# Decode attention over 65,536 keys: K transposed on VectorE in 32x32 blocks of bf16 pairs, scores and V as 512-column products, 32 KB load rows

## Chip, cores, metric

One core of a Trainium2 chip. The metric is device microseconds (us) per execution. One of the runs of the kernel before took 745 us, far from all others; it is in no ratio, but it is one of the four behind the median of 707.1 us below. In the profiles, PE is TensorE's products, PEld its weight loads, DVE VectorE, ACT ScalarE, SPq the sync engine's queue that issues the loads. PSUM is the memory that the kernels' products are written to and added up in. Of a product's two operands the code calls the stationary one (the weights) lhsT and the moving one rhs. L148 is a line of the kernel's file.

## The reference, cut

```python
B, Hq, Hkv, Sq, Sk, D = 1, 32, 8, 1, 65536, 128          # all bf16
k = jnp.repeat(k, 4, axis=1); v = jnp.repeat(v, 4, axis=1)
scores = jnp.einsum("bhqd,bhkd->bhqk", q, k) * D ** -0.5
out    = jnp.einsum("bhqk,bhkd->bhqd", softmax(scores), v)
```

One query per head, eight groups of four heads. Each group reads 16.8 MB of K and 16.8 MB of V, 268.4 MB in all, and does little arithmetic with them. K arrives with keys on the partitions. In both kernels a product contracts over the partitions of its two operands, and the score product contracts over d, so both transpose K.

## The kernel before

K and V are read in blocks of 16,384 keys (4 MB) into four shared buffers. For each K block TensorE makes 128 transposes, VectorE copies them out of PSUM eight at a time, and TensorE makes 128 products with four columns each. For each V block it makes 128 more. In the source, K blocks of one group are interleaved with V blocks of the group before it, eight chunks of 128 keys at a time.

```python
KB = 16384; T = 32; CB = 4                 # a partition's share of a block: 4 runs of 32 keys = 4 x 8 KB
iopool = tc.tile_pool(name="iopool", bufs=4)            # K and V blocks share the buffers
nc.sync.dma_start(out=kn, in_=k[0, g, b*KB:(b+1)*KB, :].rearrange("(c p t) d -> p c t d", p=P, t=T))
# K step, per 8 chunks
for i in range(8):
    nc.tensor.transpose(out=pt[:, i*P:(i+1)*P], in_=kn[:, c, t0+i, :], identity=ident_bf)   # L148
nc.vector.tensor_copy(out=kTn, in_=pt)                                                      # L154
for i in range(8):
    nc.tensor.matmul(out=sc[:, 4*jj:4*jj+4], lhsT=kTn[:, i*P:(i+1)*P], rhs=qT_g)            # L157
# V step, per chunk
nc.tensor.matmul(out=psum_oT, lhsT=vb[:, c, t, :], rhs=E_g[:, 4*j:4*j+4])                   # L195
# ... cut: maximum over the group, exp on ScalarE, row sums, normalisation at the end
```

## Time and profile before

| | before |
|---|---|
| time, us | 706.9 (703.7 to 707.3 without the outlier) |
| span of the profiled run, us | 705.8 |
| mean load rate over the span | 380 GB/s |
| load rate while loads are queued | 425 GB/s |
| PE / DVE busy | 80% / 56% |

Three lines of the profile's page: the share of 16 DMA engines and the rate in 40 equal slices of the span, and the chain of waits, by engine. The chain is the work that ended last, followed back step by step to what released it.

```profile
DMA  8999799997989979899799997989979899799994
GB/s 332 427 425 425 305 405 387 386 426 327 423 356 391 426 319 425 353 397 421 308 423 377 404 420 321 423 358 425 427 309 408 360 393 423 325 413 386 425 427 202
...
PE 67%; DVE 20%; issue 6%; ACT 5%; DMA 2%; SPq 0%; DVEq 0%; ACTq 0%
```

The rate reaches 425 GB/s and then dips, deepest once in about five slices (88 us), which is once per group. Stretches of 2 us round the first group change show a dip from near. The last three columns are the granted TensorE clock (1.00 is full), the DMA share and the rate.

```profile
80.00:82.00 2.00, 1.90 (x44) 1.76 (x43) 1.77 (x4) 0.69 (x2) 0.00 (x0) 1.00 0.99 422
82.00:84.00 2.00, 2.00 (x74) 1.96 (x71) 1.21 (x3) 0.00 (x0) 0.00 (x0) 1.00 0.56 233
84.00:86.00 2.00, 2.00 (x78) 2.00 (x74) 0.00 (x0) 0.00 (x0) 0.00 (x0) 1.00 0.04 16
86.00:88.00 2.00, 2.00 (x49) 2.00 (x46) 1.38 (x2) 0.00 (x0) 0.00 (x0) 0.59 0.03 8
88.00:90.00 2.00, 1.41 (x26) 1.32 (x25) 0.97 (x2) 0.00 (x0) 0.00 (x0) 0.50 0.79 209
```

For over 4 us nothing is being read, while TensorE is busy (the first number after the comma). The waits of the queue that issues the loads say why: total us, times, longest. Each load waits for the engine that still uses its buffer.

```profile
SPq L130 <- PE psum_oT L195: 369.4, 20, 19.8
SPq L130 <- PE pt L148: 175.0, 8, 25.2
SPq L177 <- PE psum_oT L195: 59.3, 8, 18.5
```

The groups of instructions that hold TensorE and VectorE (busy us, mean ns of one, idle time before them and its releaser):

```profile
L154 DVE COPY kTn<-pt 128x1024 bf16<-128x1024 bf16 x512 | 350.0, 691 | 223.1 <-PE pt L148 214.8
L148 PE MATMUL pt<-ident_bf,kn 128*128 128x128 bf16 x4096 | 367.5, 244 | 14.5 <-DMA kn<-in_k_dram 14.5
L157 PE MATMUL sc<-qT,kTn 128*128 128x4 bf16 x4096 | 184.1, 167 | 33.8 <-DVE kTn L154 18.2
L195 PE MATMUL psum_oT<-E_g,vb 128*128 128x4 bf16 x4096 | 118.7, 166 | 26.8 <-issue 26.8
```

### The profile page before, as it was taken

The page shows a single profiled execution, that of the slowest core. Times are in us where ns is not written, and L with a number is a line of the kernel's source. Part 1 is how long each engine was busy: PE and PEld are TensorE (multiplying, and loading weights), DVE is VectorE, ACT ScalarE, POOL GpSimd, SP SyncE. Part 2 cuts the span into 40 slices and gives each one's busy share as a digit, 9 for nine tenths or more (in the row PEclk, how much of TensorE's full clock was granted, in tenths as well). Part 3 has the DMA queues.
Part 4 walks back from the last instruction along what each step waited for, and adds up shares of the span by engine and source line. Part 5 has one row for each costly group of instructions (what it writes and reads, how often), then busy time and mean ns, then how long its engine had stood idle before and what let it go on. Part 6 is the DMA issues. An engine that isn't in the chain of part 4 may idle for free.

```text
span 705.8 us, 26009 instructions
## 1 busy us (share of the span) xinstructions
PE 562.4 (80%) x12337; PEld 505.3 (72%) x12337; DVE 396.7 (56%) x595; ACT 41.9 (6%) x65; POOL 0.8 (0%) x7
## 2 busy tenths in 40 slices
PE   1998898839988499884999849998498984999945
PEld 1777887738877388773888738888387873888845
DVE  1888666536565365653656536566265662656620
ACT  0000200020000200002000020000200002000020
POOL 0000000000000000000000000000000000000000
PEclk9999788868988678876788768788578885789755
DMA  8999799997989979899799997989979899799994
GB/s 332 427 425 425 305 405 387 386 426 327 423 356 391 426 319 425 353 397 421 308 423 377 404 420 321 423 358 425 427 309 408 360 393 423 325 413 386 425 427 202
DMA packets 34011, 270.12 MB, mean 383 GB/s; under 512 B 1136, under 2 KB 1136, under 8 KB 1136
## 3 DMA queue, kind: packets, MB, share of 16 engines
q1 hardware_dynamic: 33904, 268.46, 91.9%
q8 instruction: 96, 1.57, 0.8%
q14 instruction: 11, 0.09, 0.0%
HBM read 268.44 MB, written 0.01 MB: 380 GB/s over the span
## 4 chain that ended last, share of the span: by engine, by line
PE 67%; DVE 20%; issue 6%; ACT 5%; DMA 2%; SPq 0%; DVEq 0%; ACTq 0%
PE pt L148 34%; PE sc L157 17%; DVE kTn L154 15%; PE psum_oT L195 15%; ACT E_g L106 5%; DVE mx L88 3%; DMA kn<-in_k_dram 2%; DVE S_g L168 1%; PE psum_b L98 1%; PE psum_lb L116 1%; PE psum_t L90 0%; PE psum_mrow L94 0%; DVE nmb L102 0%; SPq L66 0%; DVE mrow L96 0%
## 5 line engine op out<-in xcount | busy, mean ns | idle before, releaser
L154 DVE COPY kTn<-pt 128x1024 bf16<-128x1024 bf16 x512 | 350.0, 691 | 223.1 <-PE pt L148 214.8
L148 PE MATMUL pt<-ident_bf,kn 128*128 128x128 bf16 x4096 | 367.5, 244 | 14.5 <-DMA kn<-in_k_dram 14.5
L148 PEld LDWEIGHTS <-kn 128*128 128x128 bf16 x4096 | 281.6, 109 | 14.5 <-DMA kn<-in_k_dram 14.5
L157 PE MATMUL sc<-qT,kTn 128*128 128x4 bf16 x4096 | 184.1, 167 | 33.8 <-DVE kTn L154 18.2
L157 PEld LDWEIGHTS <-kTn 128*128 128x128 bf16 x4096 | 145.8, 99 | 84.2 <-DVE kTn L154 75.9
L195 PE MATMUL psum_oT<-E_g,vb 128*128 128x4 bf16 x4096 | 118.7, 166 | 26.8 <-issue 26.8
L195 PEld LDWEIGHTS <-vb 128*128 128x128 bf16 x4096 | 114.2, 99 | 28.8 <-issue 28.8
L106 ACT ACTIVATE E_g<-S_g,nmb 128x512 bf16<-128x512 bf16 x32 | 40.6, 1416 | 641.0 <-DVE nmb L102 641.0
L116 PE MATMUL psum_lb<-lsum_all,ones_mat 128*128 128x4 f32 x16 | 4.4, 349 | 37.9 <-ACT E_g L106 37.9
L116 PEld LDWEIGHTS psum_lb<-lsum_all,ones_mat 128*128 128x128 f32 x16 | 3.8, 295 | 38.6 <-ACT E_g L106 38.6
L168 DVE CAST S_g<-sc 128x512 bf16<-128x512 f32 x32 | 22.1, 690 | 12.5 <-PE sc L157 12.5
L123 DVE RECIPROCAL rl_all<-psum_lb 128x4 f32<-128x4 f32 x8 | 1.5, 181 | 40.5 <-PE psum_lb L116 40.5
L90 PE MATMUL psum_t<-ident,mx 128*4 128x128 f32 x8 | 2.9, 360 | 23.2 <-DVE mx L88 23.2
L88 DVE TENSOR_REDUCE mx<-S_g 128x4 f32<-128x2048 bf16 x8 | 18.3, 2284 | 0.2
L90 PEld LDWEIGHTS psum_t<-ident,mx 128*4 128x4 f32 x8 | 0.6, 81 | 23.9 <-DVE mx L88 22.3
L205 DVE TENSOR_TENSOR oT_all<-psum_oT,rl_all 128x4 bf16<-128x4 f32 x8 | 1.2, 153 | 18.1 <-PE psum_oT L195 18.1
L106 ACT ACTIVATION_READ_ACCUMULATOR E_g<-S_g,nmb 128x1 f32 x32 | 8.0, 251 | 0.0
L98 PE MATMUL psum_b<-mrow,ones_row 1*128 1x4 f32 x16 | 4.7, 361 | 1.7 <-DVE mrow L96 1.7
L98 PEld LDWEIGHTS psum_b<-mrow,ones_row 1*128 1x128 f32 x16 | 4.0, 308 | 2.4 <-DVE mrow L96 2.3
L102 DVE TENSOR_SCALAR nmb<-psum_b 128x4 f32<-128x4 f32 x8 | 1.3, 163 | 5.3 <-PE psum_b L98 5.2
L96 DVE COPY mrow<-psum_mrow 1x4 f32<-1x4 f32 x8 | 1.2, 150 | 1.9 <-PE psum_mrow L94 1.8
L106 ACT ACT_TABLE_LOAD x1 | 1.3, 1283 | 0.7 <-PEq L265 0.7
(36 smaller groups left out, 6.2 us busy)
## 6 DMA issues: line engine op xcount, KB each, us to landing
kn<-in_k_dram SPq DMA_DIRECT2D x32, 4096.0 KB, 14.0
vb<-in_v_dram SPq DMA_DIRECT2D x32, 4096.0 KB, 23.1
qT<-in_q_dram SPq DMA_TRANSPOSE x1, 2.3
out_dram<-o_sb SPq DMA_DIRECT2D x1, 8.0 KB, 1.4
```

Source lines behind the costliest of these rows:

```text
L88: nc.vector.tensor_reduce(out=mx[:, :], in_=S_view, axis=AX.X, op=ALU.max)
L90: nc.tensor.transpose(out=psum_t[:, :], in_=mx[:, :], identity=ident[:, :])
L98: nc.tensor.matmul(out=psum_b[:, :], lhsT=ones_row[:, :], rhs=mrow[:, :], start=True, stop=True)
L102: nc.vector.tensor_scalar_mul(out=nmb[:, :], in0=psum_b[:, :], scalar1=-SCALE)
L106: nc.scalar.activation(out=E_view[:, h, :], in_=S_view[:, h, :], func=ACT.Exp, bias=nmb[:, h:h + 1], scale=SCALE, accum_out=lsum_all[:, g ...
L116: nc.tensor.matmul(out=psum_lb[:, :], lhsT=ones_mat[:, :], rhs=lsum_all[:, g * HPG:(g + 1) * HPG], start=True, stop=True,)
L123: nc.vector.reciprocal(out=rl_all[:, g * HPG:(g + 1) * HPG], in_=psum_lb[:, :])
L148: nc.tensor.transpose(out=pt[:, i * P:(i + 1) * P], in_=self.kn[:, c, t, :], identity=ident_bf[:, :],)
L154: nc.vector.tensor_copy(out=kTn[:, :], in_=pt[:, :])
L157: nc.tensor.matmul(out=self.sc[:, jj * HPG:(jj + 1) * HPG], lhsT=kTn[:, i * P:(i + 1) * P], rhs=qT_g, start=True, stop=True,)
L168: nc.vector.tensor_copy(out=S_g[:, c0:c0 + CKB * HPG], in_=self.sc[:, :])
L195: nc.tensor.matmul(out=psum_oT[:, :], lhsT=self.vb[:, c, t, :], rhs=E_g[:, j * HPG:(j + 1) * HPG], start=(j == 0), stop=(j == C - 1),)
```

## The change

The intent is to take the transposes off TensorE and to give it few wide products.

- VectorE transposes K in 32x32 blocks, reading two bf16 values as one 32-bit word. Afterwards partition r of each quarter of the partitions holds the pair of d values that belongs to r; the four quarters hold different keys.
- The weights are q, placed block-diagonally in zeros: each quarter of the rows has q in its own four of 32 columns. The window into the zero-padded array shifts by four columns per 16 keys, so 32 products of 512 columns add up in one PSUM tile with 128 useful rows.
- The exponentials are transposed in 32x32 blocks too and become a stationary operand with 16 columns. V is the moving operand with 512 columns. Four products go to four column strips of the array. A mask and a small product collect the useful quarter of the result.
- A load gives each partition one run of 32 KB in place of four of 8 KB, and the last V block comes in five shrinking pieces.
- K and V blocks are no longer interleaved: the four K blocks of a group are followed by its own four V blocks.

```diff
-    pt = pst.tile([P, NW * P], bf16)            # K: 128 transposes, 16 copies, 128 products a block
-    nc.tensor.transpose(out=pt[:, i*P:(i+1)*P], in_=self.kn[:, c, t, :], identity=ident_bf)
-    nc.vector.tensor_copy(out=kTn[:, :], in_=pt[:, :])
-    nc.tensor.matmul(out=self.sc[:, jj*HPG:(jj+1)*HPG], lhsT=kTn[:, i*P:(i+1)*P], rhs=qT_g)
+    nc.vector.transpose(out=kt[:, :],           # K: 4 of these and 32 products a block
+        in_=kn[:, t0:t0+TS, :].rearrange("p t d -> p (t d)").bitcast(u32))                  # L112
+    nc.tensor.matmul(out=sc[:, :], lhsT=wz[:, g, s, w, 28-4*gp:28-4*gp+P],                  # L121
+        rhs=ktb[:, u:u+16, s, :, w], start=(n == 0), stop=(n == 31))
...
-    nc.tensor.matmul(out=psum_oT, lhsT=self.vb[:, c, t, :], rhs=E_g[:, j*HPG:(j+1)*HPG])
+    nc.tensor.matmul(out=vacc[32*c:32*c+4*ng, 0:ng*D], lhsT=et[:, b, o:o+4*ng],             # L179
+        rhs=vt.rearrange("p (y t) d -> p y t d", t=16)[:, gp0:gp0+ng, tt, :])  # c = tt % 4
...
-    in_=k[...].rearrange("(c p t) d -> p c t d", p=P, t=32)
+    in_=k[...].rearrange("(p t) d -> p t d", p=P)
```

## The prediction

> **What bounds the kernel now.** The inputs are 268.4 MB (DMA table). While loads are queued DMA is full at 424-428 GB/s (windows of 10 us, 20 to 60 us), so reading alone needs 268.4/0.4255 = 631 us. The span is 705.8 us. The missing 75 us: about 3 us of start, 9 us of tail (data stop near 697 us; the last V products, normalisation and store follow), and some 60 us in which DMA has nothing queued. In windows of 2 us round a group change (72-176 us) the DMA share falls to 0.03-0.04 at 84-88 us, and dips again near 109, 131 and 173 us: 5-6 us at the group change, about 2 us at block changes. The sync queue's waits name the cause: loads wait for buffers that TensorE holds (K loads on psum_oT 369 us, on pt 175 us). The chain of waits is PE 67%, DVE 20%, DMA 2%. In the K-only stretch PE is busy 9.0 of 10 us, with DVE copies of 691 ns between. TensorE, through buffer release, opens the gaps.
>
> **What the change does.** Removed: 4096 PE transposes (367 us busy), 512 PSUM copies (350 us), 4096 + 4096 products with N=4, 32 score evictions (22 us).
>
> Added, estimates:
> - VectorE: 4 transposes of 128x2048 32-bit words per K block. A reduction over 2048 elements takes 2284 ns in this trace; [...]the same: 9.1 us a block. The maximum (0.7 us) stands in VectorE's program before the next block's transposes and waits for TensorE's last 8 products[...].
> - TensorE: 32 score products N=512[...]. V: 32 products per block in four column strips[...].
>
> Per group: [...]8 loads of 9.85 us = 79 us. Four 4 MB buffers give 30 us of slack[...]. So I expect DMA never without a queued load, the compute waiting for DMA, and nearly all 60 us of gaps gone. The start gains 1 us (no q transpose ahead of the first K load); the tail shrinks to about 4 us, since the last V block comes in five shrinking pieces.
>
> **Time.** 2.7 (start) + 631 + 3.7 (last 8 products, scale, store) + 1 (time over span) = 639 us, about 10% faster. Range 633-658. Faster 0.94, same 0.04, slower 0.02.
>
> **What would show it.** DMA share 1.0 in every slice but the ends; mean about 421 GB/s; the chain mostly DMA; kt transposes about 2.28 us;[...] VectorE busy 55-60%, PE under half.
>
> **What would make it wrong.** A 32-bit transpose at half rate (4.5 us)[...]. Score products slowed by the moving operand's step of two bf16 values[...]. Column strips that do not overlap, at half clock:[...] gaps return. Loads of 32 KB rows below 425 GB/s: each 1% costs 6 us.

The 9.1 us, four times 2284 ns, are the author's estimate. The compute of a group was a sum of K, softmax, V and collection. It came to 64-84 us, against 79 us for the eight loads. The sum for the time: 2.7 + 631 + 3.7 + 1 is 638.4, given as 639. Its 3.7 us are an estimate too; in the trace of the kernel before it is 3.3 us from the last V product (702.5 us) to the end of the span (705.8 us).

## More of the kernel before

Times are medians of several runs.

Most of that waiting is harmless, since other loads are still in flight. But a K and a V block are worked on together, so their buffers come free together (the sync queue issues a K load at 108.64 us and a V load at 109.10 us, the next two at 128.38 and 128.84 us), and only two loads are then in flight. A gap opens where a pair of blocks takes TensorE longer than two loads.

## The result, and the profile after

| | before | after |
|---|---|---|
| time, us (before: median of all four runs, the outlier among them) | 707.1 | 635.3 (634.5 to 636.1) |
| ratio | 1 | 0.898 (0.895 to 0.901) |
| span, us | 705.8 | 634.2 |
| load rate while loads are queued | 425 GB/s | 430 GB/s |
| PE / DVE busy | 80% / 56% | 60% / 56% |

A ratio is the mean time of one kernel's fast runs over that of the other's fast runs of the same rounds, so it is not quite the ratio of the medians. Intervals are 95%.

The same three lines of the page after:

```profile
DMA  8999999999999999999999999999999999999995
GB/s 366 430 436 433 437 434 432 429 430 429 432 430 431 430 429 432 430 429 430 429 430 430 429 432 431 432 435 430 428 431 432 427 432 430 429 432 431 434 423 217
...
PE 37%; DMA 31%; DVE 24%; issue 6%; ACT 1%; ACTq 0%; SPq 0%; DVEq 0%
```

There are no dips left. Loading is what bounds the kernel, although the chain still names PE first: the chain walks through work in the order of its releases, and much of the work after a load has landed lies beside other loads. The slices, not the chain, show the bound here. The sync queue's waits that answer to those of before:

```profile
SPq L53 <- DVE kt L112: 342.0, 32, 12.6
SPq L53 <- PE vacc L179: 121.8, 28, 10.8
SPq L53 <- DMA vt<-in_v_dram: 60.8, 13, 7.4
```

They add up to 525 us against 604 before and cost nothing, as the slices show: a buffer now comes free while about three loads are still in flight. The median time from the issue of a K load to its landing is 32.4 us, which is over three loads; before it was 14.0 us. The groups that replaced those above:

```profile
L112 DVE STREAM_TRANSPOSE kt<-kn 128x2048 uint32<-128x2048 uint32 x128 | 284.4, 2278 | 23.7 <-DMA kn<-in_k_dram 23.7
L121 PE MATMUL sc<-kt,wz 128*128 128x512 bf16 x1024 | 274.4, 426 | 139.1 <-DVE kt L112 139.0
L179 PE MATMUL vacc<-vt,et 128*16 128x512 bf16 (+1 forms) x1024 | 90.5, 519 | 88.8 <-DMA vt<-in_v_dram 73.9
L134 DVE TENSOR_REDUCE mx<-sc 128x1 f32<-128x512 f32 x32 | 22.2, 692 | 74.0 <-PE sc L121 74.0
```

VectorE's timeline for two K blocks (start, us, then the operation, its count and the wait before it):

```profile
104.85 8.88 DVE L112 STREAM_TRANSPOSE kt<-kn 128x2048 uint32<-128x2048 uint32 x4
117.26 0.69 DVE L134 TENSOR_REDUCE mx<-sc 128x1 f32<-128x512 f32 x1 [3.53 <-PE sc L121]
117.87 8.88 DVE L112 STREAM_TRANSPOSE kt<-kn 128x2048 uint32<-128x2048 uint32 x4
128.92 0.69 DVE L134 TENSOR_REDUCE mx<-sc 128x1 f32<-128x512 f32 x1 [2.17 <-PE sc L121]
```

From 104.85 to 117.87 us and from there to the next transposes at 129.53 us: 13.0 and 11.7 us a K block, more than the 9.75 us of its load (4.19 MB at 430 GB/s). V blocks take TensorE 1.9 us (granted clock 1.00) to 3.6 us (granted clock 0.50), so VectorE catches up there, and the group as a whole waits for loads.

Where the 71.6 us of span went, worked out from the profiles: 268.4 MB take 631 us at 425.5 GB/s and 624 us at 430 GB/s, so 7 us are the rate; the time from the last data to the end went from about 9 us (data stop near 697 us) to 5.7 us (near 628.5 us), 3 us; the first K load is issued at 0.74 us in place of 1.97 us, 1 us; the remaining 60 us are the gaps.

### The profile page after: what moved, and what is told of

It is laid out like the page before. It is cut to its first block, busy times and chain, and to the rows that moved or that the text cites. A ratio compares the mean times of both kernels' runs of the same rounds, so it can differ in the third digit from the quotient of the medians.

```text
span 634.2 us, 4903 instructions
## 1 busy us (share of the span) xinstructions
PE 377.9 (60%) x2136; PEld 149.0 (23%) x2136; DVE 356.1 (56%) x291; ACT 24.5 (4%) x65; POOL 5.0 (1%) x7
## 4 chain that ended last, share of the span: by engine, by line
PE 37%; DMA 31%; DVE 24%; issue 6%; ACT 1%; ACTq 0%; SPq 0%; DVEq 0%
PE sc L121 32%; DMA kn<-in_k_dram 26%; DVE kt L112 21%; PE vacc L179 4%; DMA vt<-in_v_dram 3%; DMA q_in<-in_q_dram 1%; DVE mx L134 1%; ACT e L158 1%; DVE et L162 1%; PE fin L224 1%; PE pb L148 0%; DVE m L140 0%; PE pt L138 0%; DVE wz L100 0%; DVE nrow L144 0%
## 5 line engine op out<-in xcount | busy, mean ns | idle before, releaser
L121 PE MATMUL sc<-kt,wz 128*128 128x512 bf16 x1024 | 274.4, 426 | 139.1 <-DVE kt L112 139.0
L112 DVE STREAM_TRANSPOSE kt<-kn 128x2048 uint32<-128x2048 uint32 x128 | 284.4, 2278 | 23.7 <-DMA kn<-in_k_dram 23.7
L121 PEld LDWEIGHTS <-wz 128*128 128x128 bf16 x1024 | 107.6, 105 | 305.1 <-issue 214.5
L179 PE MATMUL vacc<-vt,et 128*16 128x512 bf16 (+1 forms) x1024 | 90.5, 519 | 88.8 <-DMA vt<-in_v_dram 73.9
L179 PEld LDWEIGHTS <-et 128*16 128x16 bf16 (+1 forms) x1024 | 34.1, 111 | 134.8 <-issue 108.3
L134 DVE TENSOR_REDUCE mx<-sc 128x1 f32<-128x512 f32 x32 | 22.2, 692 | 74.0 <-PE sc L121 74.0
L158 ACT ACTIVATE e<-sc,nmb 128x512 bf16<-128x512 f32 x32 | 21.7, 683 | 585.0 <-DVE nmb L153 584.1
L162 DVE STREAM_TRANSPOSE et<-e 128x512 bf16<-128x512 bf16 x32 | 22.1, 712 | 8.6 <-ACT e L158 8.6
L196 DVE TENSOR_REDUCE vs<-vm 128x128 f32<-128x512 f32 x8 | 8.2, 1019 | 0.3
L158 ACT ACTIVATION_READ_ACCUMULATOR e<-sc,nmb 128x1 f32 x32 | 6.2, 194 | 0.0
## 6 DMA issues: line engine op xcount, KB each, us to landing
kn<-in_k_dram SPq DMA_DIRECT2D x31, 4096.0 KB, 32.4
```

What stands on the lines that cost most here:

```text
L112: nc.vector.transpose(out=kt[:, :], in_=kn[:, t0:t0 + TS, :].rearrange("p t d -> p (t d)").bitcast(u32),)
L121: nc.tensor.matmul(out=sc[:, :], lhsT=wz[:, g, s, w, 28 - 4 * gp:28 - 4 * gp + P], rhs=ktb[:, u:u + 16, s, :, w], start=(n == 0), stop=(n ...
L134: nc.vector.tensor_reduce(out=mx[:, b:b + 1], in_=scs[b][:, :], axis=AX.X, op=ALU.max)
L158: nc.scalar.activation(out=e[:, :], in_=scs[b][:, :], func=ACT.Exp, bias=nmb[:, :], scale=SCALE, accum_out=ls[:, b:b + 1],)
L162: nc.vector.transpose(out=et[:, b, :], in_=e[:, :])
L179: nc.tensor.matmul(out=vacc[32 * c:32 * c + 4 * ng, 0:ng * D], lhsT=et[:, b, o:o + 4 * ng], rhs=vt[:, :, :].rearrange("p (y t) d -> p y t ...
```

## The experiments

Each is compared with the kernel before on the same chip. All gave correct results.

### 1. b_rows32: the kernel before with 32 KB rows

```diff
-    T = 32 if KB >= 32 * P else 1
+    T = 128
```

> The kernel before with 32 KB rows for K and V loads, nothing else. Theory A (the loads starve because TensorE releases buffers late, at about 20-21 us a pair of blocks and 25 us at a group change): DMA runs about 1% faster while it runs, the gaps get wider by as much, time 698-707 us. Rival B (the longer rows and with them the faster DMA carry the gain): 640-660 us.

Measured: 715.6 us, ratio 1.011 (1.005 to 1.016). The loads stream at 428 GB/s from 20 to 60 us, where the kernel before has 425, and the time got no better. Rival B falls. That it became 1% worse was outside what theory A expected. The first group takes as long as before (86.4 against 86.6 us from K issue to K issue), the later ones 88.6 against 87.9 us on average. What did grow are TensorE's waits marked "issue" among the V products (run 3 comes back to them): 36.5 us against 26.8 us in all, more than the 6.6 us between the two profiled spans. Why they grew is not shown.

### 2. b_buf5: the kernel before with five buffers

```diff
-IO_BUFS = int(os.environ.get("GQA_IOBUFS", "4"))
+IO_BUFS = int(os.environ.get("GQA_IOBUFS", "5"))
```

> The kernel before with five load buffers in place of four. Theory A (TensorE's own pace, about 87 us a group against 79 us of loads, sets the time): one more buffer delays the first gap once by up to 10 us, then the gaps are back; 695-707 us. Rival C (the prefetch was too shallow to bridge the softmax at the group change, TensorE could catch up afterwards): gaps of 5-6 us vanish, 645-665 us.

Measured: 703.6 us, ratio 0.993 (0.990 to 0.996). The rates in 40 slices:

```profile
GB/s 330 428 423 425 426 423 418 404 423 378 366 355 394 419 387 347 354 394 421 401 328 372 425 421 380 358 368 425 420 350 406 337 401 427 350 407 380 425 421 51
```

The first dip, at the fifth slice before, is gone; from the tenth slice on the dips are back. Rival C falls: a buffer delays a gap once, but TensorE never catches up.

### 3. b_vwide: the kernel before with the V half alone

```diff
-    nc.tensor.matmul(out=psum_oT, lhsT=self.vb[:, c, t, :], rhs=E_g[:, j*HPG:(j+1)*HPG])
+    nc.tensor.matmul(out=vacc[32*r:32*r+16, :], lhsT=E_g[:, j*HPG:(j+4)*HPG],   # r = (j // 4) % 4
+                     rhs=self.vb[:, c, t:t+4, :])                               # every fourth j
+    # ... and mask, sum, collecting product and scale per group, as in the changed kernel
```

> The kernel before with only the V half of the change: weights as stationary operand with 16 columns, V as 512-wide moving operand in four column strips, K path as before. Theory A says the K path (transpose on TensorE, copy on VectorE, 128 products) holds the time; V costs TensorE some 4 us a block either way: 690-710 us. Rival D (the V half carries the gain): below 665 us.

Measured: 668.2 us, ratio 0.943 (0.940 to 0.946), between the two ranges and 3 us above rival D's (run 9 shows what held it there). Theory A as I had put it fell here: I had the K path hold the time, and V cost about the same either way. One pair of a K and a V block, between two issues of K loads, first in the kernel before, then in this one:

```profile
108.65:128.40 19.75, 17.46 (x390) 15.36 (x387) 11.78 (x18) 0.00 (x0) 0.00 (x0) 0.85 0.96 394
```

```profile
103.90:120.05 16.15, 14.18 (x290) 11.27 (x288) 11.24 (x18) 0.00 (x0) 0.00 (x0) 1.00 1.01 419
```

The pair went from 19.75 to 16.15 us. Two loads take 19.7 us at 425 GB/s, so this pair alone was not behind; the group as a whole was. By the issues of their K loads the four pairs of this group took 21.2, 19.7, 20.1 and 25.6 us before, the last with the softmax: 86.6 us, against 79 us for eight loads. In this kernel they took 16.9, 16.2, 16.2 and 26.1 us, 75.4 us in all: the three faster pairs make up for the slow one. (Later groups take about 81.6 us here, since they wait for loads at 419 GB/s.) TensorE's timeline shows the V burst of that pair, before and in this kernel:

```profile
123.17 2.81 PE L195 MATMUL psum_oT<-E_g,vb 128*128 128x4 bf16 x106
127.47 0.32 PE L195 MATMUL psum_oT<-E_g,vb 128*128 128x4 bf16 x6 [1.48 <-issue]
```

```profile
117.56 1.69 PE L215 MATMUL vacc<-vb,E_g 128*16 128x512 bf16 x28
119.17 0.35 PE L178 MATMUL sc<-qT,kTn 128*128 128x4 bf16 x8
```

The burst itself is 1.1 us shorter, and 1.5 us of standing still after it are gone, a wait for which the profile names nothing ("issue", 26.8 us in all before). These waits have a pattern. The end of the chain of the kernel before shows it:

```profile
690.53 3.57 PE psum_oT L195 x128
694.10 2.37 issue
696.46 3.57 PE psum_oT L195 x128
```

Counted in the trace of the kernel before, the 22 such waits of over 0.3 us all come at the same place in TensorE's program, a multiple of 128 products (each with its weight load) apart, and each ends 2.2 to 2.5 us after a packet of the DMA queue of kind "instruction" has started. That queue moved 96 packets of 16 KB before, 72 in this kernel, 40 in run 4 and 16 in the changed kernel. That TensorE waits there for its own instructions is a guess of mine. The two kernels with 128 narrow V products a block have such waits among them (26.8 us in the kernel before, 47.0 us in run 4), the two with 32 wide ones have none. No run changed the number of instructions alone, so the guess is not shown.

The granted clock of the pair was 0.85 before and is 1.00 here: 1.00 during the burst before, 0.50 from 127.47 us on, after the standstill. No run changed one without the other.

### 4. a_vold: the changed kernel with the V half undone

```diff
-    wide(g, b, et, vt, 0, 4); wide(g, b, et, vt, 4, 4, last=(b == NB - 1))
+    for t in range(128):
+        nc.tensor.matmul(out=oT[:, :], lhsT=vt[:, t, :], rhs=et[:, b, o:o+4])
```

> The changed kernel with the V half undone: 128 products with V as stationary operand and N=4 per block, output transposed once per group. Theory A: V costs TensorE 3.4 us (26 ns each at full clock)[...] a block in place of 1.9-3.6, the group still needs only about 72 us of compute against 78 us of loads: 634-641 us. Rival D (the V half carries the gain): over 660 us.

Measured: 641.3 us, ratio 0.905 (0.902 to 0.908), a touch above the range. Rival D falls. (A figure for half clock is cut from the expectation: in the trace of the kernel before, such products follow one another 28 ns apart at a granted clock of 0.50 too, 128 in 3.57 us.) With run 3 it follows that either half alone brings more than half of the gain of 72 us, 40 us for V and 67 us for K (here with the 32 KB rows and the new order of blocks), and the two do not add: once the compute of a group is under its loads, the rest of a saving is lost in waiting. Most of the 6 us that it lacks against the changed kernel lie at the end: up to 600 us it has read 255.8 MB against 256.7 (summed from the packets), which is 2 us of loading. From 624 us on, in stretches of 4 us:

```profile
624.00:628.00 4.00, 3.56 (x128) 3.49 (x128) 0.00 (x0) 0.00 (x0) 0.00 (x0) 0.50 0.69 282
628.00:632.00 4.00, 1.98 (x75) 1.98 (x75) 0.00 (x0) 0.00 (x0) 0.00 (x0) 0.50 0.49 190
632.00:636.00 4.00, 3.55 (x134) 3.49 (x132) 0.00 (x0) 0.00 (x0) 0.00 (x0) 0.50 0.11 39
```

For some 7 us only half of the DMA engines' time is used; in the changed kernel the same state lasts about 3 us. Why the engines finish so unevenly is not shown by any view that I have.

### 5 to 7. The load rate: after_again, a_rows8, a_align

The V-half kernel read at 419 GB/s, the kernel before at 425, with the same rows. One thing that differed was where the built programs put the load buffers: at multiples of 256 bytes before, of 64 bytes in b_vwide, of 32 bytes in the changed kernel (no view of the profile shows addresses).

```diff
 a_rows8:
-    view = src[...].rearrange("(p t) d -> p t d", p=P)
+    view = src[...].rearrange("(c p t) d -> p c t d", p=P, t=32)     # four runs of 8 KB, K and V alike
 a_align:
+    pad = const.tile([P, 56], fp32)       # 224 bytes ahead of the load buffers: start at 126 x 256
+    nc.vector.memset(pad[:, :], 0.0)
```

> The changed kernel itself once more, as the base for the three small variants on the same chip: 634.5-636.5 us, 429-432 GB/s while loads stream.

> The changed kernel with the row length of the kernel before: each partition's 32 KB of a load come as four runs of 8 KB. The first call showed 425 GB/s for 8 KB rows in the kernel before (load buffers start at multiples of 256 bytes), 431 for 32 KB rows, but 419-420 for 8 KB rows in the V-half kernel, whose buffers start only at a multiple of 64 bytes. In the changed kernel they start at a multiple of 32. Theory A1 (row length and start address together set the rate): 418-421 GB/s, 647-654 us. Theory A2 (row length alone; the 419 was something else): 425 GB/s, 641-645 us. If the rate does not follow the rows: 635 us.

> The changed kernel with 224 bytes of padding ahead of the load buffers, so that they start at multiples of 256 bytes. Theory A1 ([...]a run of 32 KB is four times as long as one of 8 KB, so a quarter of 1.3%): about 0.3% faster, 633-634.5 us, 431-433 GB/s. Theory A2 (the start address does not matter): 0.0% of difference from the run of the changed kernel in this call.

Measured: 635.8 us for the changed kernel itself, 651.6 us for a_rows8 (ratio 0.919), 632.4 us for a_align (ratio 0.893). The stretch from 300 to 420 us, in that order:

```profile
300.00:420.00 120.00, 66.62 (x414) 25.68 (x407) 59.14 (x46) 2.90 (x8) 0.00 (x0) 0.76 1.00 431
```

```profile
300.00:420.00 120.00, 65.80 (x414) 24.79 (x414) 55.96 (x51) 5.79 (x16) 0.00 (x0) 0.75 1.01 420
```

```profile
300.00:420.00 120.00, 69.23 (x416) 26.46 (x409) 61.33 (x47) 2.90 (x8) 0.00 (x0) 0.75 1.00 432
```

Theory A1 holds: 8 KB rows into buffers at a multiple of 32 bytes read at 420 GB/s, in place of 431 for 32 KB rows, and cost 16 us in the kernel that is bound by loads. Padding gains 3.4 us: in windows of 1 us the last data land near 625.4 us in place of 628.4 us, which is 3.0 us of it, and the tail after them is about 5 us in both profiled runs. That is 0.5%, more than the 0.3% I had worked out from the 8 KB rows, and the time falls below my range. So the start address matters, with 32 KB rows as with 8 KB rows (8.5 us, run 9); that its cost goes by the number of runs, as the expectation took it, is not shown, since the sizes (1.3% and 0.5%) are not four to one. Multiples other than 32, 64 and 256 bytes were not tried.

### 8. a_best: padding, and TensorE kept busy at the end

In the changed kernel the last data had landed near 628.5 us, but the last product ended at 631.7 us. The granted clock was 0.50 and the small products ran at 113 ns each (24 in 2.72 us).

```diff
+    idle_work(9, prev)                    # products of 512 columns into an unused bank
     wide(g, b, et, vt, 0, 4)
+    idle_work(5, vt)
     wide(g, b, et, vt, 4, 2, last=True)
```

> The padded kernel with 14 idle products of 512 columns that fill TensorE's waits in the last 10 us, so that the granted clock is still 1.0 when the last 32 small products come (it was 0.5 in the changed kernel, 113 ns each, and the data had all landed about 2 us before they ended). Expected: the 24 + 8 small products in about 2 us in place of 3.8, 1-1.6 us less than the padded kernel, 631.5-633.5 us. If the clock does not matter there: as the padded kernel.

Measured: 631.3 us (631.2 to 631.7), ratio 0.891 (0.889 to 0.894), 0.2 us under the range; a_align in the same call 632.3 to 633.0. TensorE's timeline of the last V piece, a_align first:

```profile
624.76 2.56 PE L226 MATMUL fin<-vt,et 128*4 128x128 bf16 x24 [0.21 <-DMA vt<-in_v_dram]
627.16 0.38 PE L231 MATMUL fin<-vs,sel 128*4 128x128 f32 x2
```

```profile
624.73 1.50 PE L237 MATMUL fin<-vt,et 128*4 128x128 bf16 x24 [0.63 <-DMA vt<-in_v_dram]
626.07 0.38 PE L242 MATMUL fin<-vs,sel 128*4 128x128 f32 x2
```

The 24 products start at the same time and take 1.50 in place of 2.56 us, at a granted clock of 1.00 in place of 0.50 (624 to 627 us), and the whole run is 1.1 us shorter. This is the fastest version found, ahead of both kernels.

### 9. b_vwide_al: the V half with aligned buffers

```diff
+    pad = const.tile([P, 48], fp32)       # 192 bytes: load buffers start at 90 x 256
+    nc.vector.memset(pad[:, :], 0.0)
```

> The V-half kernel (the kernel before with only the V half of the change) with 192 bytes of padding, so that its load buffers start at multiples of 256 bytes again. Theory A1 (the start address cost it 1.3% of the load rate): 425 GB/s in place of 419-420, 658-664 us in place of 668. If the start address was not the reason: 419 GB/s and 668 us.

Measured: 659.7 us, ratio 0.932 (0.930 to 0.933), 425 GB/s from 20 to 60 us where b_vwide had 419. This settles the question of run 3's rate: 8.5 of its 668 us went with 192 bytes of padding, and the time now lies in rival D's range.

### 10. a_onestrip: all V products in one column strip

```diff
-            c = tt % 4
+            c = 0
```

> The changed kernel with all V products in the first column strip, so that no two can overlap. Theory A (a group's compute must stay under 78 us of loads; K 48 us, softmax 5 us, V now 7 us a block at full clock and up to 13.7 us at half clock in place of 1.9-3.6, collection 2 us): 83-90 us a group, 665-720 us. If the overlap of the strips did not matter: 635 us.

Measured: 678.0 us, ratio 0.957 (0.954 to 0.959). TensorE's timeline for the V blocks of one group:

```profile
149.03 3.06 PE L179 MATMUL vacc<-vt,et 128*16 128x512 bf16 x7 [1.87 <-DVE et L162]
151.98 26.28 PE L179 MATMUL vacc<-vt,et 128*16 128x512 bf16 x121
```

121 products in 26.28 us are 217 ns each. (The 7 and 13.7 us of the expectation are 32 times the spacing of the score products in the changed kernel: 217 ns at a granted clock of 1.00, 427 ns at 0.50.) With four strips, in the changed kernel, a V block's 32 products took 1.90 us at full clock, 59 ns each, 3.7 times the pace:

```profile
150.78 1.90 PE L179 MATMUL vacc<-vt,et 128*16 128x512 bf16 x32 [1.29 <-DMA vt<-in_v_dram]
```

The group grows to 83.2 us (from the first K issue to that of the next group; the group after it takes 81.7 us), over its 78 us of loads, and the time follows: eight times 4 to 5 us is about what the kernel lost, 42.7 us.

### 11. a_bf16T: K transposed as single elements

```diff
-    kt = ktp.tile([P, TS * D // 2], u32)     # 128 x 2048 words
+    kt = ktp.tile([P, TS * D], bf16)         # 128 x 4096 elements
-    rhs=ktb[:, u:u+16, s, :, w]              # every second value, 2 x 2 products
+    rhs=ktb[:, u:u+16, s, :]                 # unbroken, 4 products
```

> The changed kernel with K transposed as single bf16 elements (128x4096) in place of pairs (128x2048); as many score products, now with an unbroken moving operand. If the transpose costs by the element (712 ns for 512 bf16, 2278 ns for 2048 pairs): about 4.4 us each, a K block 20.5 us, and since the loads of the next group then wait for buffers too, 800-850 us. If it costs by the byte: 635 us. The score products' spacing should be the same[...] if the step of two elements costs nothing.

Measured: 759.2 us, ratio 1.073 (1.071 to 1.075), slower than the kernel before.

```profile
L105 DVE STREAM_TRANSPOSE kt<-kn 128x4096 bf16<-128x4096 bf16 x128 | 555.0, 4410 | 35.4 <-DMA kn<-in_k_dram 35.3
```

The transpose cost by the element here: 4410 ns for 4096, 2278 ns for 2048 words of twice the size. My range for the time was missed, because I put the wait for the maximum into every K block; in the built program VectorE takes three of the four maxima after the last transpose of the group, so a K block costs 17.3 us and not 20.5. A burst of eight score products at full clock took 1.89 us here and 1.90 us in the changed kernel, so the moving operand that steps over every second value cost nothing here.

### 12. a_buf2: two load buffers

```diff
-    iop = tc.tile_pool(name="iop", bufs=4)
+    iop = tc.tile_pool(name="iop", bufs=2)
```

> The changed kernel with two load buffers in place of four. Theory A (K blocks take 11.7 us of compute each against 9.75 us of load, so compute lags the loads by some 14 us when the softmax is done; two buffers give about 10 us of slack): gaps of about 8 us a group come back, 690-720 us, no better than the kernel before. If the prefetch depth does not matter: 635 us.

Measured: 714.5 us, ratio 1.008 (1.006 to 1.011). Its rates:

```profile
GB/s 384 323 381 364 414 432 303 372 375 422 430 303 383 369 429 424 277 385 375 440 412 333 380 378 437 362 354 353 404 439 364 354 353 403 439 334 354 353 403 274
```

A group takes 88.7 us from its first K issue to the next group's, and gaps of the same total as in the kernel before are back. The faster compute is worth nothing without the buffers that even out K blocks of 12 us and V blocks of 2 to 4 us.

## Why the prediction was right

- **What bounded the kernel before.** Right: TensorE's pace, through the release of buffers. Five buffers did not help (run 2), faster loads did not (run 1), and less work for TensorE did, in the V half (run 3) as in the K half (run 4). What I had not seen is where the time lay: in one group three pairs of blocks took 19.7 to 21.2 us, little more than the 19.7 us of their two loads, and the pair with the softmax 25.6 us. So 3.6 us off each of three pairs were enough to bring the group under its loads.
- **No gap in the loads.** Right: the slices are full but for the ends.
- **K on VectorE.** The estimate for a transpose was the 2284 ns of the reduction; measured 2278 ns, and 11.7 to 13.0 us a block. TensorE is at a granted clock of 0.50 for about 6.8 us of the longer block and 3.4 us of the other (worked out from the granted clock in stretches of 2 us), which the prediction left out; the slack hid it. Runs 11 and 12 show that both the pairs and the buffers are needed.
- **V in four strips.** The times for a V block: measured 1.9 us at full clock. Run 10 shows that without the overlap the kernel is compute-bound at 678 us.
- **Size.** 635.3 us against 639, inside the range and near its lower end. Terms of the sum were off in opposite directions, so that the total came so near is partly luck. The loads were put at 631 us, from the 425.5 GB/s of 8 KB rows; at 430 GB/s they take 624 us. I had named the rows only as a danger. The tail was put at 3.7 us and took 5.7 us from the last data, because the small products ran at half clock behind 24 others (in run 8, at full clock, it was about 3.9 us). The time over the span was put at 1 us and is 1.8 us.
- **Readings that failed.** I expected the chain to be mostly DMA and PE under half; the chain says PE 37%, DMA 31%, and PE was busy 60%, because a product of 512 columns is recorded at 426 ns on average, though eight follow one another in 1.90 us. Neither says that TensorE bounds the kernel.

## What to carry to other kernels

Compare the pace of the compute with the pace of its loads over a whole period (here a group); a group that took 10% longer than its loads opened gaps that a fifth buffer did not close, and any saving beyond the pace of the loads was worth nothing. When a kernel is bound by loads, the shape of a load is next: here long runs per partition (32 KB in place of 8 KB, 16 us less), and buffers that start at multiples of 256 bytes in place of 32 or 64 (3.4 us less with 32 KB rows, 8.5 us with 8 KB rows). VectorE's transpose cost by the element here (2278 ns for 2048 words of 32 bits, 4410 ns for 4096 bf16), so move pairs of bf16 as 32-bit words and let the product's access pattern take them apart.
